# PSUM banks dealt anew in a planned attention and MLP kernel: three for attention, one for h, attention's products ordered later

## The chip, the cores and the metric

One core of one Trainium2 chip. The metric is the device time of one execution in microseconds (us). The core has TensorE (PE, matmuls), VectorE (DVE), ScalarE (ACT), GpSimd (POOL) and SyncE (SP, which here issues nearly all DMAs). Matmuls write to PSUM, which has 8 banks.

## The reference

Windowed attention, then two feed-forward layers on its output:

```python
scores = q @ k^T / sqrt(64)             # 4 batches, 8 heads, 576 positions, head size 64
mask   = 0 <= i - j < 32                # heads 0 to 3
mask   = 0 <= i - j < 128, (i - j) % 4 == 0    # heads 4 to 7 (dilated)
attn   = softmax(where(mask, scores, -1e9)) @ v
x  = attn reordered to 2304 tokens x 512
h  = x @ w_in                           # 512 x 2048
x2 = (h * cos(h)) @ w_out               # 2048 x 512
gate = 1 / (1 + exp(-(x2 @ w_gate)))    # 512 x 1536
out  = (gate * (x2 @ w_val)) @ w_out2   # 1536 x 512
```

q, k and v are float32; the five weight matrices arrive as 64-bit floats.

## The kernel before, in words

**Numbers.** Each large product is made of three matmuls of split operands (high by low, low by high, high by high: `mm3`, L646 to L650). The weights are turned from 64-bit into two parts on the chip, by a chain on ACT, DVE and POOL (`w_tasks`, L301).

**Stages.** The tokens are cut into 6 chunks of 384 (c) and 12 groups of 192 (g). An attention block is one pair of heads of one group: 48 blocks, four per group, plain and dilated ones in turn. The first layer runs over the chunks twice, for 8 and for 8 of the 16 column blocks f of w_in: 96 steps n. A step makes h (four triples, 12 matmuls of 384 columns, into one PSUM bank), its chain, and x2 (four triples into the four `acc` banks). The second layer starts when the 96 steps are done.

**The chain of h.** `turn` (ACT, L698) reads h and rounds it to full turns, `part` (DVE, L702) reads h and takes the rest, `cosine` (ACT, L705, needs the sine table), `g` (DVE, L708) reads h again, multiplies and thereby frees the bank of h. Then `g_hi` and `g_lo` split g for x2.

**An attention block** (`attn_tasks`, L461) has four tasks on PE, each into a PSUM bank of its own: `transp` (q and k transposed, 4 matmuls, L520), `scores` (6 or 8 matmuls, L547, L549), `p_transp` (3 or 4, L578) and `pv` (12 or 16, L590). Between them stand: two copies of q and one of k out of PSUM (`q_out`, `k_out`, on ACT L537 or DVE L541), the maximum (`s_max`, DVE L557), the exponentials (`s_exp`, ACT L563, need the exp table), `s_eps` and `s_rec` (small DVE operations, L567, L570), the scaling (`s_norm`, POOL L573) and the copy of the transposed p (`p_out`, 384 elements in each of 96 or 80 partitions, ACT L537 or DVE L541; its views are `p_parts`, L580). After `pv` stand `x_hi` (ACT L602) and `x_lo` (DVE L606), which write x. The first two groups use the `acc` banks, which x2 does not need yet, all later ones the banks `a`.

**The banks before.** Four `acc`, two `h`, two `a`; when attention ends, the two `a` become two banks for the second layer (`go_late`, L1072).

**The order of the work** is made by a planner in the kernel's own Python (`Plan`, L48), an event simulation of the five engines. Every task has an engine (or two, with a duration for each), a guessed duration, a priority, buffers that it takes and gives back, and tasks that it waits for. Whenever an engine is free in the simulation, it takes the ready task with the smallest priority number whose buffers are free. A result reaches the next engine after a fixed delay (`LAT`, 0.12 to 0.255 us), a buffer after `FREE_LAT`, 0.2 us. The instructions are issued in the order that comes out, and each engine works its own list off in that order on the chip, whatever the guesses were worth. The chain of h has the smallest numbers; h and x2 of step n have n and n + 3.5; attention has numbers that lie some steps ahead of the chunk that needs it. The exponentials of a group of four blocks run as one batch, between two cosines, because each change of table loads ACT's table anew. Until the first h is issued, PE fills idle time of the plan with small `warm` matmuls (at most 400, L1080); before the change the warm tasks hold one bank of h.

## Time and profile before

| what | value |
|---|---|
| median of 3 runs | 980.5 us (977.69 to 981.04) |
| profiled execution | 977.19 us; its span, first to last instruction, 975.4 us |
| PE busy | 942.1 us (97% of the span) |
| DVE, ACT, POOL busy | 660.2, 480.0, 179.7 us |
| PE loading weights (beside its matmuls) | 886.5 us |
| mean granted PE clock | 0.99 of full speed |
| last attention work on PE | ends near 304 us |

How to read it: busy time is summed over an engine's instructions, so 97% says how full PE's list is by the profile, not that each matmul runs at its best; the end of a matmul is modelled. What matters for one part of the kernel is the share in its own stretch of time, and what PE waited for there.

### The profile page before, as it was taken

What the parts mean: (1) busy time and instruction counts of PE and PEld (TensorE: products, weight loads), DVE (VectorE), ACT (ScalarE), POOL (GpSimd) and SP (SyncE); (2) the same over time, 40 slices, a digit from 0 to 9 for tenths busy, and PEclk for the clock granted to TensorE, in tenths of its full rate; (3) what the DMA queues carried; (4) which work ended last, traced back from release to release, by engine and by line L of the source; (5) the groups of instructions that cost most, each with busy time, mean ns of one, the idle gap of its engine ahead of it and who ended that gap; (6) DMA issues with size and microseconds to landing.
All of it is one profiled execution on the core that took longest, in us unless ns stands there. A gap on an engine that the chain in (4) does not pass through costs nothing.

```text
span 975.4 us, 16434 instructions
## 1 busy us (share of the span) xinstructions
PE 942.1 (97%) x5938; PEld 886.5 (91%) x5938; DVE 660.2 (68%) x1620; ACT 480.0 (49%) x1164; POOL 179.7 (18%) x224
## 2 busy tenths in 40 slices
PE   7979999999999999999999999999999999999996
PEld 6868888898999999999999898999999999999995
DVE  7889768878777677796798686647544646444443
ACT  6778767777775555565674443324222323222222
POOL 5434222123322222332301322200000000000000
PEclk9889999999999999999999999999999999999999
DMA  7674435454332557776857899774645544644441
GB/s 177 171 200 138 152 111 152 131 157 124 102 96 94 193 198 252 271 285 238 317 196 281 319 324 367 278 302 162 216 151 190 192 172 175 230 152 151 152 152 65
DMA packets 107761, 189.82 MB, mean 195 GB/s; under 512 B 56992, under 2 KB 91040, under 8 KB 100512
## 3 DMA queue, kind: packets, MB, share of 16 engines
q1 hardware_dynamic: 106880, 188.57, 56.5%
q8 instruction: 47, 0.77, 0.3%
q10 hardware_dynamic: 800, 0.20, 0.1%
q14 instruction: 34, 0.28, 0.1%
HBM read 139.98 MB, written 48.76 MB: 194 GB/s over the span
## 4 chain that ended last, share of the span: by engine, by line
PE 85%; DVE 7%; ACT 3%; DMA 3%; issue 1%; SPq 0%; POOL 0%; ACTq 0%; DVEq 0%
PE ps_h L648 6%; PE ps_h L650 6%; PE ps_h L649 6%; PE acc L648 6%; PE acc L650 6%; PE acc L649 6%; PE oacc L1044 5%; PE oacc L1045 5%; PE oacc L1043 5%; PE ps_y L960 4%; PE ps_y L959 4%; PE ps_y L958 4%; PE ps_z L960 3%; PE ps_z L959 3%; PE ps_x L960 3%; PE ps_z L958 3%
## 5 line engine op out<-in xcount | busy, mean ns | idle before, releaser
L648 PE MATMUL acc<-gs,arena 128*128 128x384 f32 x384 | 134.0, 349 | 0.0
L648 PE MATMUL ps_h<-arena 128*128 128x384 f32 x384 | 132.6, 345 | 0.0
L650 PE MATMUL ps_h<-arena 128*128 128x384 f32 x384 | 129.0, 336 | 0.0
L649 PE MATMUL ps_h<-arena 128*128 128x384 f32 x384 | 128.8, 335 | 0.0
L650 PE MATMUL acc<-gs,arena 128*128 128x384 f32 x384 | 128.8, 335 | 0.0
L649 PE MATMUL acc<-gs,arena 128*128 128x384 f32 x384 | 128.6, 335 | 0.0
L426 POOL TENSOR_TENSOR th<-tb,th 128x512 fp32r<-128x512 f32 (+1 forms) x48 | 62.0, 1309 | 188.7 <-ACT th L421 140.6
L1043 PE MATMUL oacc<-arena 128*128 128x512 f32 x216 | 84.4, 391 | 5.1 <-DVE arena L1005 5.1
L991 ACT ACTIVATE sg<-sg 128x384 f32<-128x384 f32 x36 | 18.9, 525 | 139.6 <-DVE sg L987 139.6
L698 ACT ACTIVATE r<-ps_h 128x384 int32<-128x384 f32 x96 | 46.9, 489 | 78.7 <-PE ps_h L650 72.5
L1045 PE MATMUL oacc<-arena 128*128 128x512 f32 x216 | 85.5, 396 | 0.0
L1044 PE MATMUL oacc<-arena 128*128 128x512 f32 x216 | 85.5, 396 | 0.0
L976 DVE TENSOR_TENSOR sg<-ps_y,s 128x384 f32<-128x384 f32 x36 | 20.1, 557 | 83.4 <-PE ps_y L960 83.3
L648 PEld LDWEIGHTS ps_h<-arena 128*128 128x128 f32 x384 | 72.4, 188 | 1.0
L960 PE MATMUL ps_y<-arena 128*128 128x384 f32 x216 | 72.9, 337 | 0.0
L959 PE MATMUL ps_y<-arena 128*128 128x384 f32 x216 | 72.7, 337 | 0.0
L648 PEld LDWEIGHTS acc<-gs,arena 128*128 128x128 f32 x384 | 72.3, 188 | 0.4
L958 PE MATMUL ps_y<-arena 128*128 128x384 f32 x216 | 72.6, 336 | 0.0
L649 PEld LDWEIGHTS ps_h<-arena 128*128 128x128 f32 x384 | 72.5, 189 | 0.0
L650 PEld LDWEIGHTS ps_h<-arena 128*128 128x128 f32 x384 | 72.3, 188 | 0.0
L649 PEld LDWEIGHTS acc<-gs,arena 128*128 128x128 f32 x384 | 72.3, 188 | 0.0
L650 PEld LDWEIGHTS acc<-gs,arena 128*128 128x128 f32 x384 | 72.1, 188 | 0.0
(129 smaller groups left out, 2267.7 us busy)
## 6 DMA issues: line engine op xcount, KB each, us to landing
arena<-wd SPq DMA_DIRECT2D x36, 1792.0 KB, 7.4
wd<-th SPq DMA_DIRECT2D x12, 1792.0 KB, 6.6
wst<-in_moe_w_out_dram SPq DMA_DIRECT2D x28, 512.0 KB, 4.2
wst<-in_moe_w_in_dram SPq DMA_DIRECT2D x16, 512.0 KB, 4.1
xd<-arena SPq DMA_DIRECT2D x4, 1536.0 KB, 6.4
wst<-in_moe_w_gate_dram SPq DMA_DIRECT2D x12, 512.0 KB, 5.3
wst<-in_moe_w_val_dram SPq DMA_DIRECT2D x12, 512.0 KB, 5.8
od<-oh SPq DMA_DIRECT2D x12, 512.0 KB, 4.7
```

The lines of the kernel that those rows point to most:

```text
L426: POOL.tensor_tensor(out=t[:, 1, c], in0=wf[f][:, c].bitcast(F32), in1=t[:, 0, c].bitcast(F32), op=ALU.subtract)
L648: PE.matmul(ps, wh, xl, start=first, stop=False)
L649: PE.matmul(ps, wl, xh, start=False, stop=False)
L650: PE.matmul(ps, wh, xh, start=False, stop=last)
L698: ACT.activation(out=st["r"], in_=st["h"], func=AF.Identity, scale=INV_2PI, bias=0.25)
L958: PE.matmul(st[to], wh, xl, start=first, stop=False, **more)
L959: PE.matmul(st[to], wl, xh, start=False, stop=False, **more)
L960: PE.matmul(st[to], wh, xh, start=False, stop=kk == 1, **more)
L976: DVE.tensor_tensor(out=st[nm], in0=st[ps], in1=st[other], op=ALU.add)
L1043: PE.matmul(ps, ul, w[:, 0, :], start=f == 0, stop=False)
L1044: PE.matmul(ps, uh, w[:, 1, :], start=False, stop=False)
L1045: PE.matmul(ps, uh, w[:, 0, :], start=False, stop=f == F2 - 1)
```

## The change

1. Banks: until attention ends, one bank for h and three for attention's `a` (before: two and two). `go_late` then opens a second pool for h, and `h_tile` takes the two in turn. The plan's buffer counts follow; `late` gives the second h back. The warm tasks take no h bank from the plan any more (their tile still comes from the pool of h).
2. Order of PE's attention tasks (`SMALL`) in the plan: when the last PE task was a large one and only one attention task can run, and it was not seen as ready at an earlier decision, large tasks go first. A change between attention and large work costs 0.15 us in the plan (`SWITCH`). What other engines hand to an attention task counts as 0.5 us later, and so does a returned `a` bank (`SLACK`).
3. Guessed durations of attention's copies and small operations are replaced.
4. The copy of p runs through its elements in another order: the destination in memory order, the PSUM source with a step of two elements; before, the source in order and the destination in pairs 48 or 64 elements apart.

```diff
@@ -59,6 +59,8 @@
     LAT = {"pe": dict(pe=0, act=200, dve=200, pool=200), "act": dict(pe=230, act=210, dve=145, pool=170),
            "dve": dict(pe=255, act=130, dve=130, pool=205), "pool": dict(pe=235, act=170, dve=170, pool=120)}
     FREE_LAT = 200
+    SMALL = ("transp", "scores", "p_transp", "pv")
+    HOLD, SWITCH, SLACK = 0, 150, 500
     TABLE_LOAD = 1300
 
     def __init__(self, buffers):
@@ -92,6 +94,7 @@
             ready[e].sort(key=lambda k: self.tasks[k]["prio"])
         idle = {e: start.get(e, 0) for e in ready}
         events, now, n, left, table, port = [], 0, 0, len(self.tasks), None, 0
+        seen, turn = {}, "warm"
         for e in idle.values():
             heapq.heappush(events, (e, n, None, None))
             n += 1
@@ -119,7 +122,16 @@
             for e in ready:
                 if e is not None and idle[e] > now:
                     continue
-                for k in ready[e]:
+                small, order = False, ready[e]
+                if e == "pe":
+
+                    can = [k for k in order if k[0] in self.SMALL and all(self.free[g] >= 1 for g in self.tasks[k]["take"])]
+                    for k in can:
+                        seen.setdefault(k, now)
+                    small = turn in self.SMALL
+                    if not small and len(can) < 2 and not any(now - seen[k] > self.HOLD for k in can):
+                        order = [k for k in order if k[0] not in self.SMALL] + [k for k in order if k[0] in self.SMALL]
+                for k in order:
                     t = self.tasks[k]
                     if any(self.free[g] < 1 for g in t["take"]):
                         continue
@@ -137,6 +149,10 @@
                     for i in engines(t):
                         ready[i].remove(k)
                     dur = dur() if callable(dur) else dur
+                    if e == "pe" and dur:
+                        if (k[0] in self.SMALL) != (turn in self.SMALL):
+                            dur += self.SWITCH
+                        turn = k[0]
                     if t["table"] and t["table"] != table:
                         table = t["table"]
                         dur += self.TABLE_LOAD
@@ -157,10 +173,11 @@
                     if locks:
                         port = end
                     lat = self.LAT.get(e, {})
-                    heapq.heappush(events, (end + (t["lat"] or (self.FREE_LAT if e else 0)), n + 1, "give", k))
+                    heapq.heappush(events, (end + (t["lat"] or (self.FREE_LAT if e else 0)) + (self.SLACK if "a" in t["give"] else 0), n + 1, "give", k))
                     n += 2
                     for u in users.get((k, True), ()):
-                        heapq.heappush(events, (end + lat.get(self.tasks[u]["eng"], t["lat"]), n, "dep", u))
+                        late = self.SLACK if e and e != "pe" and u[0] in self.SMALL else 0
+                        heapq.heappush(events, (end + lat.get(self.tasks[u]["eng"], t["lat"]) + late, n, "dep", u))
                         n += 1
                     for u in users.get((k, False), ()):
                         release(u)
@@ -216,7 +233,7 @@
     wst = ctx.enter_context(tc.tile_pool(name="wst", bufs=2))
     gp = ctx.enter_context(tc.tile_pool(name="gp", bufs=2))
     accp = ctx.enter_context(tc.tile_pool(name="accp", bufs=4, space=PSUM))
-    ps_h = ctx.enter_context(tc.tile_pool(name="ps_h", bufs=2, space=PSUM))
+    ps_h = ctx.enter_context(tc.tile_pool(name="ps_h", bufs=1, space=PSUM))
     dram = ctx.enter_context(tc.tile_pool(name="dram", bufs=1, space=DRAM))
     x2d = [dram.tile([P, KD, CH], F32, name=f"x2d{c}") for c in range(NC)]
     x2h = [dram.tile([P, KD, CH], F32, name=f"x2h{c}") for c in range(NC)]
@@ -238,12 +255,18 @@
     vp = pa.enter_context(tc.tile_pool(name="vp", bufs=3))
     sp = pa.enter_context(tc.tile_pool(name="sp", bufs=2))
     smp = pa.enter_context(tc.tile_pool(name="smp", bufs=N_SM))
-    ps_a = pa.enter_context(tc.tile_pool(name="ps_a", bufs=2, space=PSUM))
-    late = {}
+    ps_a = pa.enter_context(tc.tile_pool(name="ps_a", bufs=3, space=PSUM))
+    late, turns = {}, [0]
+
+    def h_tile(name):
+
+        turns[0] += 1 if late else 0
+        pool = late["ps_h"] if turns[0] % 2 else ps_h
+        return pool.tile([P, CH], F32, tag="h", name=name)
 
     ctx.enter_context(tc.manual_schedule())
-    plan = Plan(dict(raw=2, wc=2, x=2, u=2, r=1, gs=2, o=2, xr=2, acc=4, h=2, qk=2, v=3, s=N_S, pt=2,
-                     sm=N_SM, a=2, vps=2, ob=2, tb=1, th=1, oh=1, w2=2, us=2, xt=4))
+    plan = Plan(dict(raw=2, wc=2, x=2, u=2, r=1, gs=2, o=2, xr=2, acc=4, h=1, qk=2, v=3, s=N_S, pt=2,
+                     sm=N_SM, a=3, vps=2, ob=2, tb=1, th=1, oh=1, w2=2, us=2, xt=4))
     add = plan.add
 
 
@@ -579,7 +602,7 @@
 
         def p_parts():
             st["pt"] = sp.tile([w, n, 2, nq], F32, tag="pt", name="pt")
-            return st["pt"].rearrange("p n z q -> p n q z"), st["pp"][:w].rearrange("p n (q z) -> p n q z", z=2)
+            return st["pt"], st["pp"][:w].rearrange("p n (q z) -> p n z q", z=2)
 
         def pv():
             ps = st["pv"] = pool.tile([P, 512], F32, tag=ptag, name="ps_v")
@@ -619,10 +642,10 @@
         add(("head", a), "pool", 300, head, k_war, p1, port=True)
         add(("transp", a), "pe", 340 * slow, transp, [("load_qk", half)] + last_s + q_war, p1, take=[bank], give=["qk"] if a == mates[-1] else [])
         for h in range(2):
-            add(("q_out", a, h), "dve", 265, lambda h=h: on_dve(q_parts, h), [("transp", a)] + q_war, p1,
-                alt=("act", 210, lambda h=h: on_act(q_parts, h), False))
-        add(("k_out", a), "act", 210, lambda: on_act(k_parts), [("transp", a), ("head", a)], p1,
-            alt=("dve", 265, lambda: on_dve(k_parts), False))
+            add(("q_out", a, h), "dve", 270, lambda h=h: on_dve(q_parts, h), [("transp", a)] + q_war, p1,
+                alt=("act", 345, lambda h=h: on_act(q_parts, h), False))
+        add(("k_out", a), "act", 330, lambda: on_act(k_parts), [("transp", a), ("head", a)], p1,
+            alt=("dve", 270, lambda: on_dve(k_parts), False))
         add(("t_free", a), None, 0, nothing, [("q_out", a, 0), ("q_out", a, 1), ("k_out", a)], p1, give=[bank])
         add(("scores", a), "pe", 560 * slow, scores, [("t_free", a)], p1, take=[bank, "s", "sm"])
         add(("s_max", a), "dve", 520 if plain else 600, s_max, [("scores", a)], p1, give=[bank])
@@ -630,14 +653,14 @@
         for i in range(n):
             add(("s_exp", a, i), "act", 380, lambda i=i: s_exp(i), group,
                 GS * (g - A_LEAD + (ix - ix % EG) / KD) - EXP_LEAD + ix * 1e-3 + i * 1e-4, table="exp", after=[("s_exp", a, i - 1)] if i else [])
-        add(("s_eps", a), "dve", 70, s_eps, [("s_exp", a, i) for i in range(n)], p2)
-        add(("s_rec", a), "dve", 95, s_rec, [("s_eps", a)], p2)
+        add(("s_eps", a), "dve", 130, s_eps, [("s_exp", a, i) for i in range(n)], p2)
+        add(("s_rec", a), "dve", 165, s_rec, [("s_eps", a)], p2)
         add(("s_norm", a), "pool", 640, s_norm, [("s_rec", a)], p2, give=["sm"], port=True)
         add(("p_transp", a), "pe", 340 * slow, p_transp, [("s_norm", a)], p2, take=[bank, "pt"], give=["s"])
-        add(("p_out", a), "act", 370, lambda: on_act(p_parts), [("p_transp", a)], p2, give=[bank],
-            alt=("dve", 465, lambda: on_dve(p_parts), False))
+        add(("p_out", a), "act", 480, lambda: on_act(p_parts), [("p_transp", a)], p2, give=[bank],
+            alt=("dve", 470, lambda: on_dve(p_parts), False))
         add(("pv", a), "pe", 640 * slow, pv, [("p_out", a), ("load_v", a)], p2, take=[bank], give=["pt", "v"])
-        add(("x_hi", a), "act", 210, x_hi, [("pv", a), ("x_new", c)], p2)
+        add(("x_hi", a), "act", 320, x_hi, [("pv", a), ("x_new", c)], p2)
         add(("x", a), "dve", 270, x_lo, [("x_hi", a)], p2, give=[bank])
 
 
@@ -688,7 +711,7 @@
 
         def mm_h(kk):
             if kk == 0:
-                st["h"] = ps_h.tile([P, CH], F32, tag="h", name="ps_h")
+                st["h"] = h_tile("ps_h")
             z = ORDER[kk]
             mm3(st["h"], wt["in", f], z * P, x_t[c][:, 0, z, :], x_t[c][:, 1, z, :], kk == 0, kk == KD - 1)
 
@@ -948,7 +971,7 @@
         def mm(j, kk):
             nm, b, to = PRODS[j]
             if kk == 0 and to not in st:
-                st[to] = ps_h.tile([P, CH], F32, tag="h", name="ps_" + to)
+                st[to] = h_tile("ps_" + to)
                 st["n" + to] = 0
             x, w = xs_t[s, nm], w2_t[n]
             first = st["n" + to] == 0
@@ -1071,6 +1094,7 @@
 
     def go_late():
         pa.close()
+        late["ps_h"] = ctx.enter_context(tc.tile_pool(name="ps_h2", bufs=1, space=PSUM))
         late["ps_v"] = ctx.enter_context(tc.tile_pool(name="ps_v", bufs=2, space=PSUM))
         for nm, bufs in (("tb", 1), ("th", 1), ("oh", 1), ("op", 2), ("xt", 4)):
             late[nm] = ctx.enter_context(tc.tile_pool(name=nm, bufs=bufs))
@@ -1079,18 +1103,18 @@
 
     def keep_warm(i):
         if i == 0:
-            warm["ps"] = ps_h.tile([P, CH], F32, tag="h", name="warm")
+            warm["ps"] = h_tile("warm")
         if plan.progress is None:
             PE.matmul(warm["ps"][:, :P], identb, identb, start=True, stop=True)
 
     for i in range(WARM):
         add(("warm", i), "pe", lambda: 0 if plan.progress is not None else WARM_NS, lambda i=i: keep_warm(i), prio=1e6 + i,
-            take=["h"] if i == 0 else [], give=["h"] if i == WARM - 1 else [], after=[("warm", i - 1)] if i else [])
+            after=[("warm", i - 1)] if i else [])
     for i in range(len(wseq)):
         w_tasks(i)
     for a in range(NG * KD):
         attn_tasks(a)
-    add("late", None, 0, go_late, [("x", a) for a in range(NG * KD)])
+    add("late", None, 0, go_late, [("x", a) for a in range(NG * KD)], give=["h"])
     for c in range(NC):
         x_tasks(c)
     for n in range(NSTEP):
```

## Rows read from the trace of the kernel before

**Rows 1.** The page of the profiled execution, section 1: busy us (share of the span) x instructions, by engine.

```profile
span 975.4 us, 16434 instructions
...
PE 942.1 (97%) x5938; PEld 886.5 (91%) x5938; DVE 660.2 (68%) x1620; ACT 480.0 (49%) x1164; POOL 179.7 (18%) x224
```

**Rows 2.** Busy time of each engine by stage. Columns: stretch, its length, then busy us (x instructions) of PE, PE's weight loads, DVE, ACT and POOL, granted PE clock, DMA share, GB/s.

```profile
0.00:60.00 60.00, 46.55 (x446) 40.83 (x447) 47.65 (x190) 43.30 (x146) 28.88 (x61) 0.87 0.76 194
60.00:100.00 40.00, 38.32 (x326) 34.92 (x324) 35.72 (x121) 31.59 (x80) 16.68 (x22) 0.98 0.50 142
100.00:304.00 204.00, 197.67 (x1610) 181.33 (x1608) 160.53 (x542) 145.51 (x432) 51.92 (x80) 1.00 0.43 126
304.00:536.00 232.00, 232.00 (x1341) 232.00 (x1340) 184.97 (x351) 133.12 (x265) 58.15 (x42) 1.00 0.66 238
```

**Rows 3.** Groups of PE's instructions by line from 100 to 304 us: operation, tiles, shapes, x count, then busy us, mean ns of one, and idle time before them with what ended it.

```profile
line engine op names shapes xcount | busy us, mean ns | idle before us <-releasers
...
L648 PE MATMUL acc<-gs,arena 128*128 128x384 f32 x123 | 46.3, 376 | 0.0
L648 PE MATMUL ps_h<-arena 128*128 128x384 f32 x125 | 44.2, 354 | 0.0
...
L549 PE MATMUL ps_s<-ktd,qbd 128*96 128x80 f32 x112 | 12.6, 255 | 0.8 <-DVE ktd L541 0.5 <-ACT ktd L537 0.3
L547 PE MATMUL ps_s<-ktp,qbp 128*128 128x96 f32 x84 | 12.5, 285 | 2.3 <-ACT ktp L537 0.8 <-DVE pt L541 0.4 <-DVE ktp L541 0.4
```

**Rows 4.** PE's instructions in order of time, two places from 199 to 208 us. Columns: start us, duration us, engine, line, operation, tiles, shapes, x count. L578 transposes p, L520 q and k, L590 makes the values, L549 and L547 the scores, L648 is the first of a large triple.

```profile
199.32 0.49 PE L578 MATMUL ps_p<-ident,s 96*80 96x96 f32 x4
199.66 0.33 PE L520 MATMUL ps_t<-ident,q 96*128 96x96 f32 x2
...
199.93 0.42 PE L648 MATMUL acc<-gs,arena 128*128 128x384 f32 x1
200.19 0.34 PE L649 MATMUL acc<-gs,arena 128*128 128x384 f32 x1
...
201.15 0.67 PE L590 MATMUL ps_v<-pt,vdl 80*64 80x48 f32 x16
201.75 0.91 PE L549 MATMUL ps_s<-ktd,qbd 128*96 128x80 f32 x8
202.45 0.42 PE L648 MATMUL acc<-gs,arena 128*128 128x384 f32 x1
...
207.46 0.34 PE L650 MATMUL acc<-gs,arena 128*128 128x384 f32 x1
207.87 0.91 PE L547 MATMUL ps_s<-ktp,qbp 128*128 128x96 f32 x6
```

**Rows 5.** Who waited for whom on PE from 100 to 304 us: us in total, times, longest us.

```profile
PE ps_v L590 <- DVE rs L567: 1.3, 2, 1.1
...
PE ps_s L547 <- ACT ktp L537: 0.8, 2, 0.5
```

**Rows 6.** PE in order of time: the first matmul of h in a step with a batch of exponentials, and the same five groups (20 steps) later.

```profile
149.18 0.33 PE L648 MATMUL ps_h<-arena 128*128 128x384 f32 x1
...
282.61 0.33 PE L648 MATMUL ps_h<-arena 128*128 128x384 f32 x1
```

**Rows 7.** Groups of instructions by line on ACT and DVE, whole span: the copies of p (pt), of k (ktd dilated, ktp plain), and of an x2 result (o, 384 elements, in order on both sides). Columns as in rows 3.

```profile
L537 ACT ACTIVATE pt<-ps_p 96x384 f32<-96x384 f32 x7 | 6.0, 855 | 0.2 <-PE ps_p L578 0.2
...
L779 ACT ACTIVATE o<-acc 128x384 f32<-128x384 f32 x12 | 5.8, 486 | 0.6 <-DMA x2h<-o 0.6
...
L537 ACT ACTIVATE ktd<-ps_t 128x192 f32<-128x192 f32 x15 | 5.0, 331 | 1.2 <-DVE qbd L541 0.9
...
L537 ACT ACTIVATE ktp<-ps_t 128x192 f32<-128x192 f32 x7 | 2.3, 332 | 1.4 <-DVE qbp L541 1.3
...
L541 DVE COPY pt<-ps_p 96x384 f32<-96x384 f32 x17 | 14.4, 846 | 2.7 <-PE ps_p L578 2.4
...
L777 DVE COPY o<-acc 128x384 f32<-128x384 f32 x12 | 6.6, 550 | 0.5 <-PE acc L650 0.5
```

**Rows 8.** PE, ACT and DVE in order of time, an ordinary step: first matmul of h, cosine (L705), g (L708), first matmul of the next h.

```profile
169.33 0.33 PE L648 MATMUL ps_h<-arena 128*128 128x384 f32 x1
...
173.58 0.52 ACT L705 ACTIVATE u<-u 128x384 f32<-128x384 f32 x1
...
174.14 0.56 DVE L708 TENSOR_TENSOR u<-ps_h,u 128x384 f32<-128x384 f32 x1 [0.23 <-ACT u L705]
...
175.70 0.33 PE L648 MATMUL ps_h<-arena 128*128 128x384 f32 x1
```

**Rows 9.** The same for the step with the batch of exponentials, whose h starts at 175.70, the last row of rows 8: first matmul of the next h, a small DVE operation, cosine and g of the step, g of the next step, first matmul of the h after it.

```profile
181.13 0.42 PE L648 MATMUL ps_h<-arena 128*128 128x384 f32 x1
...
182.02 1.65 DVE L567 TENSOR_SCALAR rs<-rs 128x3 f32<-128x3 f32 x1
...
184.06 0.52 ACT L705 ACTIVATE u<-u 128x384 f32<-128x384 f32 x1
...
187.04 0.55 DVE L708 TENSOR_TENSOR u<-ps_h,u 128x384 f32<-128x384 f32 x1
...
189.17 0.55 DVE L708 TENSOR_TENSOR u<-ps_h,u 128x384 f32<-128x384 f32 x1
...
190.17 0.45 PE L648 MATMUL ps_h<-arena 128*128 128x384 f32 x1
```

## The prediction

> **What bounds the kernel now.** I read the page's busy times first. TensorE (PE) is busy 942.1 of 975.4 us [rows 1], so only time that PE does not use can be won. Next the busy time by stage [rows 2]: its clock is granted almost in full from 60 us on, and from 304 to 536 us PE is busy 232.00 of 232 us with 1341 matmuls, which is 0.173 us for each, and nothing of attention is left there. What the change can move lies before 304 us, where PE idles 13.5 us in the first 60, 1.7 in the next 40 and 6.3 in the 204 after them.
>
> Idle time is not all of it, since the end of a matmul is modelled and a late start partly hides in the one before it. So I count PE's work from 100 to 304 us by start-to-start times. The lines of that stretch [rows 3] show 123 and 125 first products of a triple, so 3 x 248 = 744 large matmuls: 744 x 0.173 = 128.7 us. They also show 112/8 = 14 dilated and 84/6 = 14 plain score blocks, 28 blocks in all. The order of PE's instructions [rows 4] gives what an attention step takes when its data is there: four transposes 0.27 us (199.66 to 199.93), scores 0.70 (201.75 to 202.45), p transposed 0.34 (199.32 to 199.66), values 0.60 (201.15 to 201.75). A block is 1.91 us, and 28 of them 53.5 us. The first large matmul after a small one takes 0.26 us (199.93 to 200.19) instead of 0.173. I take some 110 such changes of kind at 0.09, or 10 us; the number of changes is my estimate from the sequence in these rows. Sum 128.7 + 53.5 + 10 = 192 of 204 us: **about 12 us are waits of attention's products for copies and reductions**. One shows in the rows: the scores at 207.87 start 0.24 us after their turn (207.46 + 0.17 = 207.63). The waits name copies and small DVE operations [rows 5].
>
> The third thing is the cadence. h starts every fourth step, always the step with a batch of exponentials, at 149.18 and five groups later at 282.61 [rows 6]: (282.61 - 149.18)/5 = 26.7 us for four steps of h and x2 and four attention blocks. By the prices above PE needs 4 x 24 x 0.173 = 16.6, plus 53.5/7.64 = 7.0 (7.64 groups in 204 us), plus 1.3 for changes of kind: 24.9 us. So 1.8 us of a group could go, 13.8 us in the stretch; that is the ceiling.
>
> **The change, part by part.** *Later order and costs.* The planner now believes that an attention product gets its data, and its bank, 0.5 us later, and prices ACT copies near what they take: 0.33 us for the k copy [rows 7], where the old table had 0.21. No instruction is added. PE's stream holds more large work ahead of each attention product, so the 12 us of waits should mostly go. The same half microsecond lets attention's chain run later, and in the first 40 us there is nothing else but warm matmuls to put in between; four hand-offs of 0.5 us bound that at 0 to +2 us, and I take **+1.0**. Queues: no DMA is added, and those on SP keep their own costs; a q load is believed 0.5 us later, but is issued by its own priority.
>
> *Exchanged loops of the copy of p.* The 48 copies take 0.855 and 0.846 us for 384 elements [rows 7]; they write pairs that lie far apart. Now they write in order and read every second element of PSUM. No row shows just that. The bounds are 0.49 to 0.55 us, an ordinary copy of 384 elements from PSUM, and 0.855, no gain. The nearest row is the dilated k copy, which reads PSUM with a step of four elements: on ACT it takes 0.331, the plain one 0.332 [rows 7]. So a step in the read costs nothing, and I take 0.52, a saving of 0.33 each. The Trainium skill ("SBUF — State Buffer", Door 1: The DMA port swizzle) says that any non-contiguous access to PSUM slows matmuls, by crossing 8-byte lines. Carried over to a copy's read, it would leave the copies near 0.85; the sum would be 976 instead of 974. The k copy's row speaks against carrying it over. After 100 us the saved time lies beside PE's work and shortens only the wait of the value products. Before 100 us DVE is busy 35.7 of 40 us [rows 2] and nearly sets the pace: 16 blocks x 0.33 = 5.3 us of copying, of which I count 40 per cent, **-2.0**.
>
> *One bank for h.* This is the part with a price. With two banks h(n+1) may start while h(n) still waits for its cosine. With one, h(n+1) waits for the product g(n). In an ordinary step h starts at 169.33 and g ends at 174.14 + 0.56 = 174.70: the bank is held 5.37 us, and the next h starts at 175.70, a full microsecond after the bank is free [rows 8]. There the second bank does nothing. In a step with the exponentials the bank is held from 175.70 to 187.04 + 0.55 = 187.59, and h of the next step starts at 181.13, 6.5 us before that [rows 9]: this overlap is lost. But 2.4 us of that hold is a stall: the cosine starts at 184.06, and in the ordinary step g ends 1.12 us after the cosine's start; here 3.53 us in DVE's order, in which an operation had stood for 1.65 us. Without it the hold is 184.06 + 1.12 - 175.70 = 9.48 us.
>
> With one bank a group cannot be shorter than 9.48 + 3 x 5.37 plus four hand-offs from g to the next h. For a hand-off the rows give 0.04 us (cosine to g, 174.10 to 174.14) to 0.45 (g at 189.17 + 0.55 = 189.72 to h at 190.17): 25.7 to 27.4 us, against 26.7 now. I take 26.1, in the lower half, because the copies of p between these steps get 0.33 us shorter. So the ceiling of 1.8 us per group becomes 0.6: 0.6 x 7.64 = **-4.6** from 100 to 304 us, and 0.6 x 1.5 = **-0.9** from 60 to 100. What fills PE between two h's: x2 of the step before (12 x 0.173 = 2.08 us) and attention's (7.0 + 1.3)/4 = 2.1 us per step. In the step with the batch the gap is 9.48 - 2.08 = 7.4 us, so PE must have work saved up there or wait. What is late next is the chain h, turn, part, cosine, g.
>
> *Three banks for attention, the switch cost and the pairing.* They give the planner freedom, and fewer changes of kind at 0.09 us. As long as h's bank sets the pace this pays nothing: 0. If it does not, it is part of the ceiling. The later return of h's second bank touches one step at 304 us: 0.
>
> **Sum.** +1.0 - 2.0 - 4.6 - 0.9 = -6.5 us. The profiled execution took 977.2 us (span 975.4), 3.3 below the median of 980.5; I take the difference from the median: **974.0**.
>
> **The rivals.**
> 1. *h's bank does not bind.* The planner fills the batch step, and only PE's own work counts: ceiling 13.8 + 1.5 x 1.8 = 16.5 us, of which some 15: about 965. For it: three of four steps have a microsecond to spare [rows 8]. Against: nothing but x2 and attention is left to fill the long hold. Chance 0.19.
> 2. *Moved, not saved.* The waits leave the small products and reappear as waits of h for g, at 26.7 us a group; or the copy stays at 0.85 us, as by the rule on PSUM lines, and DVE and ACT stay as late as they are. 977.5 to 983.5. For it: the DVE stall of 1.65 us [rows 9] waits for exponentials, which no part of the change shortens. Chance 0.20, of which 0.05 for the copy.
> 3. *Slower: h's bank is the new bound.* Place: the step with the exponentials; price: the group's loop at its upper end, 27.4 us, (27.4 - 26.7) x 7.64 = +5.3; in the first 100 us, where ACT and DVE are fuller [rows 2], holds are longer: some +2, and the later chain +1: 988. It decides from a hand-off plus queueing of 0.3 us per step on. Chance 0.25. The Trainium skill ("Perfetto Trace Analysis", Matmuls) speaks for this one: independent groups should rotate through banks, so that one is emptied while the next is filled. The row that agrees is the 6.5 us by which h starts ahead now; the rows against are the ordinary steps, where h uses no second bank.
> 4. *The forecast*, 968 to 977.5: chance 0.36.
>
> **How the numbers follow.** A difference of 0.3 per cent, 2.9 us, is about what can be told from no change. Faster: 0.36 + 0.19 = 0.55; within: 0.20; slower: 0.25. The range leaves out the far ends of cases 1 and 3: 963 to 987. The likeliest case alone is 968 to 977.5.
>
> **What would show it.** PE should hardly wait for attention's data after 60 us; instead h's first matmul should wait for DVE's g, once per four steps by 1 to 3 us. h should never start before the g of the step before has ended. The copies of p should take 0.49 to 0.56 us. The cadence should be 26.1 us, and the stretch from 304 us on stay as dense as it is. I am wrong if h starts late in the ordinary steps too (case 3), if h's waits are under half a microsecond (case 1), or if the copies stay at 0.85.

## The result and the profile after

The change makes the kernel slower: a median of 990.7 us (988.3 to 992.1), beside 980.3 for the kernel before; the ratio is 1.011, interval 1.008 to 1.014. That is +10.5 us where -6.5 was forecast, and outside the range. Ratios and intervals, here and below, are to the kernel before as it ran beside each kernel; one execution of e12, of 2210 us, is left out of its ratio. The profiled execution of the changed kernel took 988.3 us.

The page, section 1 as in [rows 1]:

```profile
span 986.5 us, 16386 instructions
...
PE 952.1 (97%) x5922; PEld 895.7 (91%) x5922; DVE 661.2 (67%) x1638; ACT 470.9 (48%) x1146; POOL 174.3 (18%) x224
```

Busy time by stage of the changed kernel, columns as in [rows 2]:

```profile
0.00:60.00 60.00, 46.45 (x407) 40.90 (x407) 45.67 (x188) 37.94 (x133) 26.61 (x58) 0.78 0.73 192
60.00:100.00 40.00, 37.17 (x285) 34.00 (x286) 36.42 (x122) 28.04 (x73) 18.89 (x25) 0.86 0.56 144
100.00:304.00 204.00, 198.21 (x1598) 182.12 (x1598) 152.88 (x542) 140.53 (x423) 48.77 (x78) 1.00 0.41 122
304.00:536.00 232.00, 231.91 (x1366) 231.01 (x1363) 189.22 (x357) 135.46 (x268) 55.97 (x43) 1.00 0.64 226
```

Look first at the granted clock (third column from the end): 0.78 and 0.86 in the first two stages, where [rows 2] have 0.87 and 0.98. And fewer matmuls were run there (warm ones among them): 407 + 285 against 446 + 326. From 100 us on the stages look alike, although PE's share "rose" from 197.67 to 198.21: busy time shows nothing of what happened.

**How the loss is counted.** For every kernel below I count the large matmuls of h and x2 that have started by 320 us, when attention's work, the same in all, is done (in e3 all but its last values); each is worth 0.173 us [rows 2]. Before: 995, after: 944, so 51 x 0.173 = 8.8 us behind. The profiled executions differ by 988.3 - 977.2 = 11.1; the other 2.3 us are lost later. For 100 us attention's matmuls count too, at the prices of [rows 4] (the task's price divided by its matmuls): 8.1 us behind. So nearly all of it is lost **before 100 us**, and the loop of h loses 0.7 instead of gaining the forecast 4.6. In the other traces this count at 320 us comes within 2.5 us of the difference between the profiled executions. Each kernel was traced in one execution. Only e10 and e16 are the same kernel in two: they differ by 0.6 us at 100 us and by 5.0 from 100 to 320 (the clock granted from 150 to 200 us was 0.93 in one and 1.00 in the other). So differences of a few us in the loop are not told by these counts alone.

PE's waits from 100 to 304 us, as in [rows 5], all rows; L671 is the first matmul of a triple, L731 is g, L570 and L572 are scores:

```profile
PE ps_h L671 <- DVE u L731: 2.9, 8, 0.6
PE ps_s L570 <- DVE ktp L564: 0.8, 1, 0.8
PE ps_s L572 <- DVE ktd L564: 0.8, 2, 0.4
PE ps_s L570 <- DVE rs L590: 0.3, 1, 0.3
```

The wait of values that led [rows 5] is gone, and so is the next one of the kernel before,

```profile
PE ps_p L578 <- DVE ktd L541: 1.2, 4, 0.5
```

and h waits for g in their place.

A group of four steps in order of time (as [rows 8, 9]): the first matmul of h, and the g that frees its bank. The first h is that of the step with the exponentials; ahead of the h of the next such step stand values (L613) and the first of six matmuls of x2; the last line is the h five groups after the first:

```profile
156.07 0.33 PE L671 MATMUL ps_h<-arena 128*128 128x384 f32 x1
...
165.43 0.56 DVE L731 TENSOR_TENSOR u<-ps_h,u 128x384 f32<-128x384 f32 x1 [0.29 <-ACT u L728]
...
166.04 0.44 PE L671 MATMUL ps_h<-arena 128*128 128x384 f32 x1
...
170.29 0.55 DVE L731 TENSOR_TENSOR u<-ps_h,u 128x384 f32<-128x384 f32 x1
...
170.90 0.45 PE L671 MATMUL ps_h<-arena 128*128 128x384 f32 x1
...
175.82 0.56 DVE L731 TENSOR_TENSOR u<-ps_h,u 128x384 f32<-128x384 f32 x1
...
176.43 0.44 PE L671 MATMUL ps_h<-arena 128*128 128x384 f32 x1 [0.28 <-DVE u L731]
...
181.25 0.56 DVE L731 TENSOR_TENSOR u<-ps_h,u 128x384 f32<-128x384 f32 x1
...
181.32 0.67 PE L613 MATMUL ps_v<-pt,vdl 80*64 80x48 f32 x16
...
181.93 0.45 PE L671 MATMUL acc<-gs,arena 128*128 128x384 f32 x1
...
183.10 0.33 PE L671 MATMUL ps_h<-arena 128*128 128x384 f32 x1
...
291.08 0.33 PE L671 MATMUL ps_h<-arena 128*128 128x384 f32 x1
```

Subtract the start of h from the end of its g: the bank is held 9.92, 4.80, 5.48 and 5.38 us, in all 25.58. From the end of a g to the next h it is 0.05, 0.06 and 0.05 us, and 1.29 ahead of the batch step: 1.45. Together 27.03, and over five groups (291.08 - 156.07)/5 = 27.0 us. Until attention ends, h never starts ahead of the g before it.

The start, PE and DVE of the changed kernel in order of time: three matmuls of h(0), g(0), the first of h(1):

```profile
37.14 0.63 PE L671 MATMUL ps_h<-arena 128*128 128x384 f32 x1
37.56 0.53 PE L672 MATMUL ps_h<-arena 128*128 128x384 f32 x1
37.88 0.53 PE L673 MATMUL ps_h<-arena 128*128 128x384 f32 x1
...
61.28 0.55 DVE L731 TENSOR_TENSOR u<-ps_h,u 128x384 f32<-128x384 f32 x1
...
62.93 0.67 PE L671 MATMUL ps_h<-arena 128*128 128x384 f32 x1
```

The same in the kernel before: h(0), then the first matmul of h(1):

```profile
38.68 0.42 PE L648 MATMUL ps_h<-arena 128*128 128x384 f32 x1
...
46.57 0.34 PE L648 MATMUL ps_h<-arena 128*128 128x384 f32 x1
```

Before, h(1) follows h(0) after 7.9 us. There h(0) holds its bank for 19.4 us, but h(1) has another. After, the bank is held from 37.14 to 61.83, and h(1) comes 25.8 us after h(0). The triple also runs at another clock: 37.56 to 37.88 is 0.32 us a matmul, not 0.173, and the clock granted from 37.5 to 38 us was 0.50, the lower of its two levels (1.2 GHz).

Two stretches of the start, in the kernel before and in the changed one (columns as in [rows 2]):

```profile
24.00:49.00 25.00, 22.67 (x220) 20.21 (x220) 20.29 (x89) 18.41 (x63) 10.56 (x15) 0.80 0.67 170
49.00:73.00 24.00, 18.32 (x155) 16.08 (x154) 20.98 (x75) 18.13 (x48) 9.55 (x14) 0.86 0.71 200
```

```profile
24.00:49.00 25.00, 22.27 (x201) 19.87 (x200) 19.12 (x85) 14.37 (x50) 9.02 (x15) 0.67 0.58 146
49.00:73.00 24.00, 19.08 (x144) 16.65 (x140) 22.88 (x75) 16.96 (x51) 10.91 (x14) 0.72 0.81 221
```

The clock falls from 0.80 to 0.67 and from 0.86 to 0.72. And PE's longest waits in the first 100 us are now:

```profile
PE ps_s L572 <- DVE ktd L564: 4.4, 5, 1.8
PE ps_s L570 <- DVE ktp L564: 3.5, 3, 1.9
...
PE ps_h L671 <- DVE arena L629: 1.9, 1, 1.9
```

The copies of p in the changed kernel, as in [rows 7]:

```profile
L564 DVE COPY pt<-ps_p 96x384 f32<-96x384 f32 x15 | 8.2, 546 | 0.1
...
L560 ACT ACTIVATE pt<-ps_p 96x384 f32<-96x384 f32 x9 | 4.3, 479 | 0.2 <-PE ps_p L601 0.2
```

0.55 and 0.48 us where [rows 7] have 0.85: what an ordinary copy of that size takes.

### The profile page after: what moved, and what is told of

Read it like the earlier page. It is cut to its first block, busy times and chain, and to the rows that moved or that the text cites. A ratio compares the mean times of both kernels' runs of the same rounds, so it can differ in the third digit from the quotient of the medians.

```text
span 986.5 us, 16386 instructions
## 1 busy us (share of the span) xinstructions
PE 952.1 (97%) x5922; PEld 895.7 (91%) x5922; DVE 661.2 (67%) x1638; ACT 470.9 (48%) x1146; POOL 174.3 (18%) x224
## 4 chain that ended last, share of the span: by engine, by line
PE 80%; DVE 11%; ACT 4%; DMA 3%; issue 2%; SPq 1%; ACTq 0%; DVEq 0%
PE ps_h L671 7%; PE ps_h L673 6%; PE ps_h L672 6%; PE acc L671 5%; PE acc L673 5%; PE acc L672 5%; PE oacc L1067 5%; PE oacc L1068 5%; PE oacc L1066 5%; PE ps_y L981 4%; PE ps_y L983 4%; PE ps_y L982 4%; PE ps_z L983 3%; PE ps_z L982 3%; PE ps_z L981 2%; PE ps_x L983 2%
## 5 line engine op out<-in xcount | busy, mean ns | idle before, releaser
L671 PE MATMUL ps_h<-arena 128*128 128x384 f32 x384 | 133.4, 347 | 5.7 <-DVE u L731 2.9
L671 PE MATMUL acc<-gs,arena 128*128 128x384 f32 x384 | 134.8, 351 | 0.0
L449 POOL TENSOR_TENSOR th<-tb,th 128x512 fp32r<-128x512 f32 (+1 forms) x48 | 59.8, 1259 | 190.3 <-ACT th L444 144.6
L725 DVE SCALAR_TENSOR_TENSOR u<-ps_h,r 128x384 f32<-128x384 f32 x96 | 53.1, 553 | 46.2 <-ACT r L721 45.4
L671 PEld LDWEIGHTS ps_h<-arena 128*128 128x128 f32 x384 | 73.0, 190 | 11.8 <-DVE u L731 8.5
L671 PEld LDWEIGHTS acc<-gs,arena 128*128 128x128 f32 x384 | 72.3, 188 | 0.9
L672 PEld LDWEIGHTS acc<-gs,arena 128*128 128x128 f32 x384 | 72.4, 189 | 0.0
```

What stands on the lines that cost most here:

```text
L449: POOL.tensor_tensor(out=t[:, 1, c], in0=wf[f][:, c].bitcast(F32), in1=t[:, 0, c].bitcast(F32), op=ALU.subtract)
L671: PE.matmul(ps, wh, xl, start=first, stop=False)
L672: PE.matmul(ps, wl, xh, start=False, stop=False)
L725: DVE.scalar_tensor_tensor(st["u"], st["h"], INV_2PI, st["r"], op0=ALU.mult, op1=ALU.subtract)
```

## The experiments

**The theory:** h's single bank is the cost. **The rivals:** the later order costs it (in the start, where little else can run); or the pairing of attention's products does; or the planner's order just came out worse, as it might after any change. The first five runs undo or add one part; the next three complete the eight combinations of banks, pairing and later order; the rest ask where in time a part costs, and how much is chance of the order. "By 100 us" and "100 to 320" are work of PE ahead (+) or behind (-) of the kernel before, counted as above; "after 280" is the part of the second that falls from 280 to 320 us, where attention's last blocks run. e3 and e9 to e16 stand below.

| kernel | median us | ratio [interval] | by 100 us | 100 to 320 | after 280 |
|---|---|---|---|---|---|
| copy, durations (e4) | 974.6 | 0.996 [0.994, 0.998] | -0.2 | +5.9 | +0.2 |
| + later order (e6) | 979.0 | 1.000 [0.998, 1.001] | -7.1 | +7.4 | 0.0 |
| + pairing (e7) | 991.1 | 1.013 [1.010, 1.016] | -7.5 | -3.8 | -1.4 |
| + both (e1) | 983.9 | 1.005 [1.003, 1.006] | -5.8 | +0.4 | -0.8 |
| + banks (e5) | 989.3 | 1.011 [1.008, 1.014] | -2.4 | -10.9 | -6.7 |
| + banks, later order (e8) | 996.3 | 1.018 [1.014, 1.022] | -8.3 | -6.9 | -6.4 |
| + banks, pairing (e2) | 994.8 | 1.016 [1.014, 1.018] | -14.2 | -3.7 | -2.3 |
| + all three: the change | 990.7 | 1.011 [1.008, 1.014] | -8.1 | -0.7 | -1.2 |

**e1: the change, with the banks as before.**

```diff
-... ps_h ... bufs=1   ... ps_a ... bufs=3   Plan(... h=1 ... a=3)
+... ps_h ... bufs=2   ... ps_a ... bufs=2   Plan(... h=2 ... a=2)
```

> The changed kernel with the banks put back to two for h and two for attention; later order, pairing, durations and the exchanged copy stay. Theory 1, one bank for h costs the time (h(1) waits for the bank from 52.6 to 62.9 us, and PE's work by 100 us is 8 us behind): most of the 11 us comes back, 979 to 982 us, and the second h starts near 47 us again. Theory 2, the later order of attention's products costs it (h of step 0 takes 15.4 us instead of 7.9 because x of its last parts comes late): 987 to 991 us, and the first h stays that long.

(With the banks, the warm tasks hold one bank of h in the plan again.) 983.9 us, between the two theories: 6.8 us come back, but the start stays 5.8 us behind. One bank alone is not the cause.

**e2: the change without the later order.**

```diff
-    HOLD, SWITCH, SLACK = 0, 150, 500
+    HOLD, SWITCH, SLACK = 0, 150, 0
```

> The changed kernel with the half microsecond taken out of the plan (a product's data and banks count as before), all else as changed. Theory 1: 988 to 991 us, as the changed kernel. Theory 2: 978 to 983 us, and the first h takes 8 us again.

994.8 us, slower than either theory said. Beside one bank for h and the pairing the later order is worth 4 us, and the start is 14.2 us behind without it, 8.1 with it; it is not what made the change slow as a whole.

**e3: the kernel before, with the new banks alone** (the edit is that of e1 the other way round, with `h_tile` and the later return).

> The kernel before with the banks alone: three for attention, one for h until attention ends, no change in the planner's rules or durations, old copy. Theory 1: 987 to 991 us. Theory 2: 978 to 983 us.

997.7 us, the worst of all and beyond both theories: +18.7 for the banks alone.

**e4: the kernel before, with the copy exchanged and the new durations.**

```diff
-            return st["pt"].rearrange("p n z q -> p n q z"), ...rearrange("p n (q z) -> p n q z", z=2)
+            return st["pt"], ...rearrange("p n (q z) -> p n z q", z=2)
```

> The kernel before with the exchanged copy and the new durations alone: banks and planner's rules as before. Both theories: the copies take 0.48 to 0.55 us instead of 0.85, PE's waits of attention shrink by a third (4 of 12 us), 975 to 979 us. If the order that comes out of the new durations is itself the harm: over 983 us.

974.6 us, faster than both kernels. Its h of a batch step, and the one five groups later:

```profile
147.26 0.33 PE L671 MATMUL ps_h<-arena 128*128 128x384 f32 x1
...
276.91 0.33 PE L671 MATMUL ps_h<-arena 128*128 128x384 f32 x1
```

(276.91 - 147.26)/5 = 25.9 us a group, against 26.7 [rows 6]: with two banks the cadence that was forecast is reached by the copy and the durations.

**e5: the same with the new banks.** The edit is that of e3.

> Banks three and one, exchanged copy, new durations; the planner's rules (half a microsecond later, pairing with switch cost) stay as before. If the parts add up, banks +18.7 and copy with durations -4.4 give 993 to 995 us, and the two rules together then bring 4 us with one bank for h. If the copy and durations are worth more where h's chain sets the pace (one bank), 985 to 990 us, and the rules bring nothing.

989.3 us. From e4 to e5 only the banks change: 0.015 of 979, or **14.7 us**. The same two h as in e4:

```profile
157.71 0.35 PE L671 MATMUL ps_h<-arena 128*128 128x384 f32 x1
...
295.22 0.45 PE L671 MATMUL ps_h<-arena 128*128 128x384 f32 x1 [0.30 <-DVE u L731]
```

27.5 us a group, 1.6 more than in e4. Yet h itself waits little: from 150 to 280 us I add up how much later than the price of the task before it each task of PE starts (prices of [rows 4], 0.26 us for the first large matmul after a small one). Ahead of h that is 0.9 us (e4: 0.4), ahead of attention's products 13.5 (e4: 5.0), and 9.1 of these stand between the batch step's h and the next (e4: 1.1). So the lost overlap shows up as waits of the products that must now fill the batch step: from its h to the next takes 10.5 us on average instead of 5.5, and the other three steps together give back 3.5 of that.

Over a third of the work that e5 loses against e4 is lost elsewhere, where attention ends. The stretch from 300 to 310 us in e5, in e8 (the change without the pairing, below) and in the change (columns as in [rows 2]):

```profile
300.00:310.00 10.00, 8.73 (x68) 7.67 (x69) 5.54 (x17) 6.72 (x22) 3.38 (x4) 0.66 0.41 122
```

```profile
300.00:310.00 10.00, 7.47 (x55) 6.10 (x54) 5.47 (x18) 7.26 (x28) 4.05 (x5) 0.75 0.39 119
```

```profile
300.00:310.00 10.00, 9.95 (x94) 8.70 (x92) 7.23 (x16) 6.09 (x15) 0.61 (x2) 1.00 0.36 123
```

PE idles there and its clock is granted at 0.66 and 0.75; with the pairing (the change) neither happens.

**e6: e4 with the later order.**

```diff
-                    heapq.heappush(events, (end + lat.get(...), n, "dep", u))
+                    late = self.SLACK if e and e != "pe" and u[0] in self.SMALL else 0
+                    heapq.heappush(events, (end + lat.get(...) + late, n, "dep", u))
```

> Two banks each, exchanged copy, new durations and the half microsecond alone (no pairing, no switch cost). With both rules this stood at 983.9 us, with neither at 974.6. If the half microsecond is what harms, 981 to 985 us and the first 60 us fall behind by 2 us of PE work; if it only removes waits, 971 to 975 us.

979.0 us. It does what it says in the loop (waits ahead of attention's products 2.6 us instead of 5.0), and the start is 7.1 us behind.

**e7: e4 with the pairing and the switch cost.**

```diff
+                    if not small and len(can) < 2 and not any(now - seen[k] > self.HOLD for k in can):
+                        order = [large tasks first]
...
+                            dur += self.SWITCH
```

> Two banks each, exchanged copy, new durations, the pairing rule and the switch cost of 0.15 us, without the half microsecond. If the pairing is what harms (attention's products stand behind a large one where attention gates the work, as in the first 100 us), 981 to 985 us; if the half microsecond is, 973 to 976 us.

991.1 us, above both ranges: with two banks the pairing is the dearest part, in the start (-7.5) and in the loop, 9.7 us below e4. PE's waits in e4 from 150 to 280 us, all rows, and the first five of e7:

```profile
PE ps_p L601 <- DVE ktd L564: 1.4, 4, 0.7
PE ps_s L570 <- DVE rs L590: 0.3, 2, 0.2
```

```profile
PE ps_s L570 <- DVE ktp L564: 1.4, 2, 1.0
PE ps_p L601 <- DVE arena L629: 1.2, 4, 0.4
PE ps_s L572 <- ACT ktd L560: 0.9, 2, 0.7
PE ps_s L570 <- ACT arena L625: 0.8, 2, 0.4
PE ps_s L572 <- DVE ktd L564: 0.6, 2, 0.3
```

1.7 us of waits become 4.9 in these rows. And PE returns from small to large work 52 times in that stretch, against 48 in e4 (53 in the kernel before): the changes of kind that the rule prices have not become fewer.

**e8: the change without pairing and switch cost.**

```diff
-    HOLD, SWITCH, SLACK = 0, 150, 500
+    HOLD, SWITCH, SLACK = 0, 0, 500
...
-                    if not small and len(can) < 2 and ...
+                    if False:
```

> The changed kernel without the pairing rule and the switch cost; banks three and one, the half microsecond, copy and durations stay. Pairing harmful: 984 to 988 us; pairing useful where h has one bank (it keeps large work in front): 993 to 998 us.

996.3 us. The part that costs 7 us of the loop beside two banks (e6 to e1, 9.7 from e4 to e7) gains 6.2 beside one (-6.9 to -0.7), and 5.2 of that after 280 us. The costs of the parts don't add.

**e9: the change, both rules for attention's blocks from the ninth on only.**

```diff
-  ... k[0] in self.SMALL and all(...)          ... u[0] in self.SMALL else 0
+  ... k[0] in self.SMALL and k[1] >= 8 and all(...)   ... u[0] in self.SMALL and u[1] >= 8 else 0
...
-  if (k[0] in self.SMALL) != (turn in self.SMALL):
+  if self.progress is not None and (k[0] in self.SMALL) != (turn in self.SMALL):
```

The last line lets the switch cost count only once the first h is issued: in the plan the warm matmuls are large work, so in the change both the switch cost and the pairing count in the start, too, where they put warm matmuls ahead of a lone attention task.

> The changed kernel, but the half microsecond on results and the pairing rule hold only for attention blocks from the third group on (the first eight blocks, which gate the first h, are ordered as before); banks three and one. If the rules harm by stretching the start: PE's work by 100 us is 3 us behind the two-bank kernel with copy and durations (as with the banks and no rules) instead of 8, and the total falls to 983 to 987 us. If the start is lost to the single bank of h itself: 988 to 992 us, unchanged.

988.2 us, with an interval that overlaps the change's. In its trace the start wins back 3.4 us (-4.7), the loop loses as much (-4.1). At one place, from the h at 204.98 to the one four steps later at 236.4 us, a group takes 31.4 us: a cosine is there, and the g that belongs to it (L728, L731) comes more than 2 us later, behind attention's copies and a piece of a weight's chain in DVE's list:

```profile
213.08 0.52 ACT L728 ACTIVATE u<-u 128x384 f32<-128x384 f32 x1
...
215.91 0.55 DVE L731 TENSOR_TENSOR u<-ps_h,u 128x384 f32<-128x384 f32 x1
```

Why the plan lets that happen is open.

**e10: e4 with the later order from the ninth block on.** The edit is the `u[1] >= 8` of e9 in e6.

> Two banks each, exchanged copy, new durations, the half microsecond only for blocks from the third group on, no pairing. If the half microsecond harms only in the start: 972 to 976 us, the start as without it. If it harms anywhere: 978 to 981 us, as with it everywhere.

971.7 us (ratio 0.993, interval 0.990 to 0.995), the lowest median, and 7 us below e6, from which it differs in the first eight blocks alone; e16 repeats it.

**e11: e4 with one guess moved by 5 ns**, to see what a reshuffled order is worth by itself.

```diff
-        add(("s_max", a), "dve", 520 if plain else 600, ...
+        add(("s_max", a), "dve", 525 if plain else 605, ...
```

> Control: exchanged copy and new durations as in the fourth run (974.6 us), only the guessed duration of the maximum made 5 ns longer, which no instruction feels. It shows how much the time moves when the planner's order is merely shaken. If effects of 2 to 4 us are order by chance, it lies 2 us or more from 974.6; if the order is robust, within 1.5 us.

975.1 us (0.996, interval 0.994 to 0.997) against 974.6, though hundreds of PE's instructions stand elsewhere in its list. This one reshuffle is worth half a microsecond, which speaks against the 5 to 20 us above being such chance; it is one sample and no proof.

**e12: the kernel before with the exchanged copy alone.** The edit is the diff of e4, without the durations.

> The kernel before with the exchanged copy alone, guessed durations as before (0.37 and 0.465 us for it, so the guess becomes nearly true). Copy the cause of the 4.4 us: 974 to 977 us. New durations the cause: 978 to 980 us.

974.7 us (0.995, interval 0.993 to 0.997): the whole gain of e4. The durations add nothing that can be told. Its copies:

```profile
L564 DVE COPY pt<-ps_p 96x384 f32<-96x384 f32 x17 | 9.3, 546 | 2.5 <-PE ps_p L601 2.4
...
L560 ACT ACTIVATE pt<-ps_p 96x384 f32<-96x384 f32 x7 | 3.4, 481 | 0.2 <-PE ps_p L601 0.2
```

**e13: e5 with two banks for attention**, so that one bank stands empty.

```diff
-... ps_a ... bufs=3   Plan(... a=3)
+... ps_a ... bufs=2   Plan(... a=2)
```

> One bank for h, two for attention, one bank unused until attention ends; exchanged copy and new durations, no new rules. With three attention banks this stood at 989.3 us, with two and two at 974.6. If the missing bank of h is the whole price and attention's third bank gives nothing back: 988 to 991 us. If the third bank gives back part of the price: 993 us or more.

991.6 us (1.013, interval 1.010 to 1.016), 2 more than e5, with intervals that overlap. What attention's third bank gives back is some 2 us and not clear of the noise; the cost is that h lost its own. It need not show in the cadence: in e13 a group takes 26.3 us, less than in the kernel before, and its trace is 8.6 us behind by 100 us and loses another 5.3 after 280 us.

**e14: e4 with the later order in the first eight blocks only** (`u[1] < 8` in e6, and no delay for returned banks).

> Two banks each, exchanged copy, new durations, the half microsecond on results for the first eight attention blocks only. If the half microsecond stretches the start and does nothing bad later: PE's work at 100 us 7 to 9 us behind the kernel without it, total 978 to 982 us. If not the start: 973 to 976 us.

977.5 us (0.998, interval 0.996 to 1.000); 4.9 us behind by 100 us, less than expected. By its time alone it is not to be told from e4. With e10 and e16, which keep the later order out of the first eight blocks and whose medians lose nothing, it places the cost of the later order beside two banks in the start.

**e15: e9 with the banks, too, as before until the h of step 7**, when h's second bank is handed to attention.

```diff
+    add(("swap",), None, 0, swap_banks, [("h", 7, KD - 1)], take=["h"], give=["a"])
```

> Two banks for h and two for attention up to h of step 7, then one and three as in the changed kernel; both rules only for blocks from the third group on; copy and durations as changed. If one bank for h costs by its own loop in the steady stretch: the start is 2 to 3 us behind the best start, and from 100 to 320 us 7 to 10 us are lost against two banks, 981 to 985 us. If the price of the banks lies in the start alone: 972 to 976 us.

989.5 us (1.010, interval 1.008 to 1.013). h(1) is back at 47.1 us, but by 100 us the kernel is 4.6 behind and by 320 another 5. PE's largest wait from 150 to 280 us (L683 and L743 are here h and g):

```profile
PE ps_h L683 <- DVE u L743: 1.8, 5, 0.6
```

That is above both ranges. Sparing the first blocks does not rescue the change; h waits for g as in the change itself.

**e16: e10 once more.**

> The kernel with the half microsecond after the start only, again (971.7 us in the first three rounds, against 974.6 without it). If the gain is real: 970 to 973 us, below 0.995 of the kernel before; if it was chance: 974 to 977 us.

973.5 us (0.995, interval 0.993 to 0.997). Faster than both kernels, but not to be told from the copy alone.

## Why the prediction was wrong

**The copy: right in mechanism, too small.** 0.52 us was taken, 0.48 and 0.55 measured; the saving was put at 2.0 us, and alone it is 4.9 (0.005 of 979, interval 3.3 to 6.6). By the count of e12 the start's share was nearly right (2.5 us by 100 us); the assumption that after 100 us it "shortens only the wait of the value products" and so belongs to another term was the error: 2.2 us more come from there. The k copy's row was the right neighbour. The Trainium skill ("SBUF — State Buffer", Door 1: The DMA port swizzle), carried over to this read, would have left the copy near 0.85; the trace does not agree.

**The first 100 us: the largest miss.** Forecast was a gain, 1.0 - 2.0 - 0.9 = -1.9; measured 8.1 behind, so 10.0 us. The two rules of the planner, later order and pairing, put the start back by 5.6 us beside two banks (e4 to e1) and by 5.7 beside one (e5 to the change); the bank puts it back by 2.2 (e4 to e5) and 2.3 (e1 to the change). The forecast had a gain of 0.9 from the loop here, nothing for the pairing, nothing against the bank, and +1.0 for the later order. (A mere reshuffle, e4 to e11, moves this count by 1.2.) Within the pair the parts don't add: each alone takes 7 us beside two banks (e6, e7), and in the change itself the later order helps, since without it the start is 14.2 behind (e2).

**Later order in the start: wrong.** "0 to +2 us, and I take +1.0" came from four hand-offs of 0.5 us. Measured beside two banks: 4.7 us behind e4 with this part in the start alone (e14), 6.9 with all of it (e6). The half microsecond does more than delay a chain: it changes which task the plan takes, and from there the order (as e11 shows for 5 ns). By what path that costs 5 to 7 us is open.

**What the start looks like.** h(0) is stretched between attention's products, its bank is held 24.7 us, h(1) waits for it, PE waits 7.9 us for copies of k, and the clock granted is lower. The clock goes with the loss: over the first 100 us it was granted at 0.80 to 0.86 in the seven kernels that are 7 us or more behind by then (the change 0.81), and at 0.88 to 0.97 in the others. Which of these is cause and which is consequence the runs do not separate.

**The loop of h: the mechanism right, the size off.** The holds were forecast as 9.48 + 3 x 5.37 = 25.59 and measured as 25.58. Of the hand-offs I took 0.5 in all and chose "the lower half"; they are 1.45: three at the lower bound, and 1.29 us ahead of the batch step, where PE finishes values and x2 while the bank is free. So 27.0 instead of 26.1: 0.9 x 7.64 = 6.9 us by the cadence. By the count of work it is 5.3 (-0.7 instead of +4.6), and another 2.3 us are lost after 320 us: -6.5 + 10.0 + 5.3 + 2.3 = +11.1, the difference of the profiled executions. The row against rival 3, "the ordinary steps, where h uses no second bank", was weighed wrongly: the loss is in the batch step. In [rows 9] h starts 6.5 us ahead there; that overlap paid for the exponentials. From the batch step's h to the next takes 10.3 us on average in the change instead of 5.7, and the two steps after it give back 4.3. (In the kernel before the second bank also serves the step after the batch step in three of five groups, by 0.4 to 1.1 us; [rows 9] happen to show one of the other two.)

**Three banks, pairing and switch cost at 0: wrong.** The third bank is worth some 2 us, not clear of the noise (e5, e13). The pairing costs 7 to 10 us of the loop beside two banks (e6 to e1, e4 to e7) and gains 6 to 7 beside one (e8 to the change, e5 to e2), most of it after 280 us. There are 80 returns from small to large work from 100 to 304 us in the kernel before, not the estimated 110. In the change, pairing and later order together win back 10.2 us of the loop that the bank costs (-10.9 to -0.7), and lose 5.7 in the start. So the change as a whole hardly differs from e5 (990.7, 989.3).

**The rivals.** Rival 1 (h's bank does not bind) fell: h starts 0.05 or 0.06 us after g in 14 of 20 steps, ordinary ones among them, which was the sign named for rival 3. Rival 2 (moved, not saved) describes the loop: from e5 to the change the waits ahead of attention's products fall from 13.5 to 5.2 us, those ahead of h rise from 0.9 to 5.1. Rival 3 gave side and size (988), but partly by luck, with a wrong split: 5.3 us for the loop, where the cadence rose by 0.3 x 7.64 = 2.3, and 3 for the start, where 8.1 went. The bank's own price depends on the rules beside it: 14.7 to 18.7 us without the pairing (e4 to e5, e6 to e8, the kernel before to e3), 3.7 with it (e7 to e2), and 6.8 in the change (e1), near the 7.3 that rival 3 put on the bank. In all five pairs the kernel with one bank is the slower, e7 to e2 alone with intervals that overlap. The Trainium skill ("Perfetto Trace Analysis", Matmuls) says that independent groups should rotate through banks; e4 against e5 agrees, at 14.7 us.

**Open:** why the pairing lengthens the waits of attention's products beside two banks; why the plan puts the batch step's h 0.8 to 1.6 us behind its free bank; why the two rules together put the start back, and what part the clock has in it; why the kernels with one bank and no pairing lose 5 to 7 us where attention ends.

## What to carry to other kernels

A spare buffer that is idle in two or three steps of four can still carry the longest one: ask what it overlaps in the longest step, not how often it is used. In a kernel whose order comes from a planner, a part's price depends on the others; measure it with each of them there and away, and take the part that stands by itself (here the copy, 974.7 us) alone.

## What the runs showed of the hardware

A copy from PSUM of 384 elements in each of 96 partitions that reads every second element and writes in order takes 0.48 us on ACT and 0.55 on DVE, as the plain ones do [rows 7] (0.486 and 0.550 in 128 partitions); the same copy that reads in order and writes pairs far apart takes 0.85 on both. So here the write's order costs and the read's does not. From the end of DVE's g to PE's first matmul into the freed bank it took 0.05 or 0.06 us in 14 of 20 steps of the change.
